# Attention into a two-layer MLP on one core: a new order of the first loads, weight conversions among the first heads, and four times as many products of zeros ahead of the fourth pair

## The chip, the cores and the metric

The kernel runs on one core of a Trainium2 chip. The metric is the device time of one execution in microseconds (us); a kernel's time is the median of its runs. Lower is better. Names used below: PE is the matrix engine (TensorE), ACT the scalar engine, DVE the vector engine, POOL the GpSimd engine, SP the engine whose queue issues nearly all loads and stores. PSUM is the memory of eight banks into which PE writes.

## The reference, cut to what matters

```python
# q, k, v: 8 batches, 8 heads, 576 positions, 64 per head, float32
scores = q @ k.T / 8                                   # per batch and head
mask_local   = (0 <= i - j) & (i - j < 32)             # heads 0 to 3
mask_strided = (0 <= i - j) & (i % 32 == j % 32)       # heads 4 to 7
attn = softmax(where(mask, scores, -1e9)) @ v
x = attn.transpose(0, 2, 1, 3).reshape(4608, 512)      # tokens x model
h = maximum(x @ w_in, 0)                               # 512 x 2048
y = (h * h) @ w_out                                    # 2048 x 512
```

All of it is float32 to the accuracy of float32.

## The kernel before, in words

The 4608 tokens are cut into 12 chunks of 384. For each chunk the attention of its tokens is written into four tiles: xlh and xll (local heads, high and low part), xsh and xsl (strided heads). A float32 number is split into a high part that the matrix engine takes as it is and a low part, the rest; a product of two such numbers is three matmuls. The MLP of a chunk walks over 16 tiles of the hidden layer. `up` (L430) makes a tile h of 128 hidden units by 384 tokens in 12 matmuls, four parts of x by three products; ACT then takes relu, square and the high part gh (L435, L436, L437), DVE the low part gl (L438). `down` (L450) adds the tile into three PSUM banks y in nine matmuls, six with gh and three with gl. PE works at `up` of tile s and `down` of tile s - 2 in turn, while the other engines do the attention of the next chunk: local heads by `pe_head` (L214 and L216 split keys and queries, L231 scores, L240 exponentials, L245 scaling, L273 products with v), strided heads on POOL and DVE (L380, L381, L402, L403).

The weights come in 16 pieces, alternately of w_in and w_out. `fetch(k)` loads piece k (the first twelve in one load of 1 MB, 128 x 1024 numbers of two words), and `convert()` makes its high and low part from two 32-bit words of each number: a scaling of the whole piece on ACT (L150), and then for each half an ACT pass into a PSUM bank (L162, into a bank of `zbank`), two DVE passes (L165, L166), an ACT cast (L169, the high part) and a POOL subtraction (L170, the low part). The cast and the subtraction of a half are written behind the ACT pass of the half after it.

Chunk 0 has nothing to overlap with, so its heads are worked out in four pairs by `pe_pair`: first[0] and first[1] are the local heads, late[0] and late[1] (the third and the fourth pair) the strided ones with their tokens sorted. A pair runs in steps, and a `next` of its generator writes one step: the loads of qk and v; the scores (L308, 8 products into two PSUM banks) with mask and row minimum on DVE (L312, L313); the subtraction on POOL (L316), exponential on ACT (L317), sum on DVE (L318), reciprocal (L320) and scaling on POOL (L322); the transposes on PE (L327) with their copies on ACT (L328); the products with v (L335 local, L346 strided); and the split into x (L350 on ACT, L351 on DVE). In the names below, b_0_1_200 and b_0_1_201 are the two banks of first[0], b_1_1 those of first[1], b_0_0 those of late[0] and b_1_0 those of late[1]; the e tiles are named in the same way, and the last number only tells tiles apart.

`zeros(bank, n)` (L525) has PE multiply zeros n times; nothing reads the result. Before the first pair it does 60 of these, after the first two pairs' scores 30, and ahead of the fourth pair's scores 30 more.

What sets the order: each engine works its own program in order. A scheduler places the instructions of the source into these programs by a model of durations, so the order in a program is not that of the source. `tc.issue_after(x)` and `behind(...)` keep what is written inside from being placed before x. Loads of SP's queue are issued in program order; the first loads hold, in KB, qk of a local pair 416, v of a local pair 256, qk of a strided pair 384, v of a strided pair 192, a piece of weights 1024, and on ACT's queue the masks 256 and the identity 64.

Of the kernel before, what the change touches and what calls it, by code (L numbers as in the profile page):

```python
# [12 lines left out]
ALU = mybir.AluOpType  # L13
AX = mybir.AxisListType
# [14 lines left out]
QC = 96  # L29
# [9 lines left out]
NWARM = 60  # L39

NEARLY = 3
# [6 lines left out]
def f32(ap):  # L48
    return ap.bitcast(F32)
# [11 lines left out]
def windows(c):  # L61

    res, at = [], 0
    for b, g in SEGS[c]:
        for qc in (2 * g, 2 * g + 1):
            if res and res[-1][:2] != (b, qc - 1):
                at += STR
            res.append((b, qc, at))
            at += QC
    return res  # L70
# [14 lines left out]
def attn_moe(ctx: ExitStack, tc, qk_l, v_l, qk_d, v_d, qk_p, v_p, f_s, q_s, k_s, v_s, w_in, w_out, masks, eye, out):  # L85
    nc = tc.nc
# [13 lines left out]
    def psum(i, nm):  # L100

        return ps.tile([P, 512], F32, name=nm, tag=f"ps{i}")
# [16 lines left out]
    last = {}  # L119
# [4 lines left out]
        order += [(p, 0), (p - 1, 1)]  # L124
    order.append((NFT // 2 - 1, 1))
    wi, wo, raws = {}, {}, {}
    zbank, zturn = (2, 3), iter(range(1000))

    def fetch(k):

        p, which = order[k]
        src = (w_out if which else w_in)[p].bitcast(U32).rearrange("p (n t) -> p n t", t=2)
        if k < 12:
            raw = wpool.tile([P, 1024, 2], U32, name=f"raw{k}", tag=f"w{k + 8 if k < 8 else k + 4}")
            nc.sync.dma_start(out=raw, in_=src)
            raws[k] = [(raw, slice(0, 1024))]
        else:
            raws[k] = []
            for i in range(0, 1024, WP):
                raw = spool.tile([P, WP, 2], U32, name=f"raw{k}_{i}", tag="s3", bufs=5)  # L140
                nc.sync.dma_start(out=raw, in_=src[:, i : i + WP])
                raws[k].append((raw, slice(i, i + WP)))
# [40 lines left out]
    def x_tiles(c):  # L183
        if c not in xt:
            xt[c] = {
                (kind, part): xpool.tile([P, 2, TC], F32R, name=f"x{kind}{part}{c}", tag=f"x{kind}{part}")
                for kind in "ls"
                for part in "hl"
            }
        return xt[c]  # L190
# [94 lines left out]
    def pe_pair(c, pr, local, qk, vr, es, pt, banks, sm):  # L285

        u = f"{c}_{pr}_{int(local)}"
        if local:
            kw, wins, nv = KW, [at for _, _, at in windows(c)], P
            src, vsrc = qk_d[c, pr], v_d[c, pr]  # L290
            mk = mask_sb[:QC, 0:2, :].rearrange("p w k -> p (w k)").unsqueeze(1).broadcast_to([QC, 2, 2 * KW])
        else:
            kw, wins, nv = QC, [QC * w for w in range(NW)], QC
            src, vsrc = qk_p[pr], v_p[pr]
            mk = mask_sb[:QC, 3, :QC].unsqueeze(1).broadcast_to([QC, NW, QC])
        nk = wins[-1] + kw
        nc.sync.dma_start(out=qk[:, : TC + nk], in_=src[:, : TC + nk])
        last["s"] = nc.sync.dma_start(out=vr[:nv], in_=vsrc)
        yield
        v4 = vr.rearrange("p (h w d) -> p h w d", h=2, w=NW)  # L300
        nm = small.tile([P, 2, NW], F32, name=f"nm{u}", tag="nm")
        rs = small.tile([P, 2, NW], F32, name=f"rs{u}", tag="rs")
        ss, s_ps = sums[sm], [banks() for _ in range(2)]
        e4 = [e[:QC, : NW * kw].rearrange("p (w k) -> p w k", k=kw) for e in es]
        for w in range(NW):
            for h in range(2):
                rows = slice(D * h, D * (h + 1))
                last["p"] = nc.tensor.matmul(s_ps[h][:QC, w * kw : (w + 1) * kw], qk[rows, w * QC : (w + 1) * QC], qk[rows, TC + wins[w] : TC + wins[w] + kw], start=True, stop=True)  # L308
        for h in range(2):

            flat = (lambda t: t[:, : NW * kw].rearrange("p (g k) -> p g k", g=mk.shape[1]))
            nc.vector.scalar_tensor_tensor(out=flat(es[h][:QC]), in0=flat(s_ps[h][:QC]), scalar=-SCALE, in1=mk, op0=ALU.mult, op1=ALU.subtract)  # L312
            nc.vector.tensor_reduce(out=nm[:QC, h], in_=e4[h], op=ALU.min, axis=AX.X)  # L313
        yield
        for h in range(2):
            nc.gpsimd.tensor_sub(e4[h], e4[h], nm[:QC, h].unsqueeze(2).broadcast_to([QC, NW, kw]))  # L316
            last["a"] = nc.scalar.activation(e4[h], e4[h], AF.Exp, scale=-1.0)  # L317
            nc.vector.tensor_reduce(out=ss[:QC, NW * h : NW * (h + 1), 0], in_=e4[h], op=ALU.add, axis=AX.X)  # L318
        nc.vector.tensor_reduce(out=rs[:QC].rearrange("p h w -> p (h w)"), in_=ss[:QC], op=ALU.add, axis=AX.X)
        last["v"] = nc.vector.reciprocal(rs[:QC], rs[:QC])  # L320
        for h in range(2):
            last["g"] = nc.gpsimd.tensor_mul(e4[h], e4[h], rs[:QC, h].unsqueeze(2).broadcast_to([QC, NW, kw]))  # L322
        yield
        p4 = pt.rearrange("p (h w q) -> p h w q", h=2, w=NW)
        for h in range(2):
            for w in range(NW):
                nc.tensor.transpose(s_ps[h][:kw, w * QC : (w + 1) * QC], e4[h][:, w], ident[:QC, :QC])  # L327
            last["a"] = nc.scalar.copy(pt[:kw, h * TC : (h + 1) * TC], s_ps[h][:kw, :TC])  # L328
        yield
        x = x_tiles(c)  # L330
        if local:
            o = s_ps[0]
            for w in range(NW):
                for h in range(2):
                    nc.tensor.matmul(o[D * h : D * (h + 1), w * QC : (w + 1) * QC], v4[:kw, h, w], p4[:kw, h, w], start=True, stop=True)  # L335
            outs = [(o[:, :TC], [x["l", s][:, pr, :] for s in "hl"])]
        else:

            r0 = D * pr
            outs = []  # L340
            for a in range(2):
                o = s_ps[a]
                for w in range(NW):
                    for h in range(2):
                        p0 = r0 + STR * h
                        nc.tensor.matmul(o[p0 : p0 + STR, w * QC : (w + 1) * QC], v4[:kw, h, w, STR * a : STR * (a + 1)], p4[:kw, h, w], start=True, stop=True)  # L346
                by_i = lambda t: t[r0 : r0 + D].rearrange("p (s i r) -> p s i r", s=2, r=STR)
                outs.append((o[r0 : r0 + D, :TC].rearrange("p (s r i) -> p s i r", s=2, i=SI), [by_i(x["s", s][:, a, :]) for s in "hl"]))
        for src, (xh, xl) in outs:
            last["a"] = nc.scalar.copy(xh, src)  # L350
            last["v"] = nc.vector.tensor_sub(xl, src, f32(xh))  # L351
        yield
# [109 lines left out]
    def behind(ins, gen):  # L462

        while True:
            with ExitStack() as st:
                for i in ins.values():
                    st.enter_context(tc.issue_after(i.ins))
                try:
                    k = next(gen)
                except StopIteration:  # L470
                    return
            yield k
# [39 lines left out]
    ungated = convert()  # L512

    late = [pair_at(0, pr, False, 2 + pr, ("y0", "14")[pr]) for pr in range(2)]
    first = [pair_at(0, pr, True, pr, ("23", "yy")[pr]) for pr in range(2)]
# [6 lines left out]
    def zeros(bank, n):  # L522
        w_ps = psum(bank, f"w_ps{bank}")
        for _ in range(n):
            nc.tensor.matmul(w_ps[:, :P], warm, warm, start=True, stop=True)  # L525

    zeros(0, NWARM)
    next(first[0])
    next(first[1])
    nc.scalar.dma_start(out=mask_sb, in_=masks)  # L530
    nc.scalar.dma_start(out=ident, in_=eye)
    next(late[0])
    next(late[1])
    for k in range(NEARLY):
        fetch(k)
    next(first[0])
    next(first[1])
    with tc.issue_after(last["p"].ins):
        zeros(0, NWARM // 2)
        for k in range(NEARLY, 8):  # L540
            fetch(k)
    next(late[0])
    with tc.issue_after(last["p"].ins):
        zeros(1, NWARM // 2)
    next(first[0])
    next(first[1])
    weights = behind({"a": last["a"]}, ungated)
    next(late[1])
    for i in range(2):
        next(first[0])  # L550
        next(first[1])
        next(late[0])
        next(late[1])
        if i:
            weights = behind({"a": last["a"]}, ungated)
        else:
            for _ in range(2 * NEARLY):
                next(weights)
    next(late[0])
    next(late[1])  # L560
# [1 line left out]
    zbank = (2,)  # L562

    NS = NCHUNK * NFT
    for s in range(NS + 2):
        c, j = divmod(s, NFT)
# [8 lines left out]
        if c + 1 < NCHUNK:  # L575
# [11 lines left out]
            while ds < fs * cost:  # L587
                k = next(st, "end")
# [82 lines left out]
```

## Time and profile before

| what | value |
|---|---|
| median of 3 runs | 903.63 us (903.14 to 903.86) |
| the profiled execution | 902.66 us |
| span of its instructions | 900.8 us |
| PE busy | 886.3 us, 98% |
| POOL, DVE, ACT busy | 693.4, 669.5, 564.4 us |
| TensorE clock granted, mean of the span | 0.982 |

The span runs from the first to the last instruction; the profiled execution is 1.86 us longer, and it is 0.97 us below the median. Busy shares are averages over the span; a wait shows as "idle before" an instruction, with the instruction that released it behind an arrow. A clock of 1.00 is full speed, 0.50 half.

### The profile page before, as it was taken

How to read it: one execution, taken by the hardware profiler on the slowest of the kernel's cores; microseconds unless marked ns; L12 is line 12 of the kernel's file. 1: busy time of each engine (PE TensorE's matmuls, PEld its weight loads, DVE VectorE, ACT ScalarE, POOL GpSimd, SP SyncE). 2: the span in 40 equal slices, each digit the busy share in tenths (PEclk: the TensorE clock that was granted, in tenths of full speed). 3: DMA queues.
4: the chain of work that ended last, by engine and by line, in shares of the span. 5: the costliest groups of instructions: out<-in, count | busy, mean ns of one | idle time of the engine just before them, and what ended most of it. 6: DMA issues, size and time to landing. Idle time of an engine off the chain costs nothing.

```text
span 900.8 us, 14866 instructions
## 1 busy us (share of the span) xinstructions
PE 886.3 (98%) x4744; PEld 800.0 (89%) x4744; DVE 669.5 (74%) x1840; ACT 564.4 (63%) x1458; POOL 693.4 (77%) x724
## 2 busy tenths in 40 slices
PE   8989999999999999999999999999999999999997
PEld 7778899999999999999989989999999999999996
DVE  6789668878877878878878887887886887885111
ACT  3898967657657657747746755755665765764332
POOL 5788577788788889989879997988899799785000
PEclk8599999999999999999999999999999999999999
DMA  9833441323113114102212311221131111000000
GB/s 352 346 123 126 129 150 35 121 69 104 51 51 112 47 48 139 43 13 98 75 32 69 104 31 54 59 86 60 28 110 47 46 46 68 25 1 2 35 1 35
DMA packets 26798, 71.41 MB, mean 79 GB/s; under 512 B 2976, under 2 KB 8736, under 8 KB 25184
## 3 DMA queue, kind: packets, MB, share of 16 engines
q1 hardware_dynamic: 26432, 70.14, 23.4%
q8 instruction: 37, 0.61, 0.3%
q10 hardware_dynamic: 288, 0.33, 0.1%
q14 instruction: 41, 0.34, 0.1%
HBM read 61.01 MB, written 9.44 MB: 78 GB/s over the span
## 4 chain that ended last, share of the span: by engine, by line
PE 86%; POOL 5%; DVE 5%; ACT 2%; issue 1%; DVEq 0%; POOLq 0%; ACTq 0%
PE h L430 41%; PE y L450 40%; POOL pp L402 2%; PE s L231 2%; PE o L273 2%; POOL pq L380 1%; DVE sc L381 1%; DVE px L263 1%; PE b L308 1%; DVE p_t L256 1%; PE w_ps L525 1%; PE b L335 0%; POOL kx L215 0%; DVE e L312 0%; DVE nm L313 0%
## 5 line engine op out<-in xcount | busy, mean ns | idle before, releaser
L450 PE MATMUL y<-w,gh 128*128 128x512 f32 x1152 | 361.9, 395 | 2.4 <-ACT gh L437 2.4
L450 PEld LDWEIGHTS y<-w,gh 128*128 128x128 f32 x1152 | 212.6, 189 | 35.0 <-ACT gh L437 2.6
L430 PE MATMUL h<-xlh,w 128*128 128x384 f32 x768 | 232.7, 342 | 0.4 <-DVE xsl L351 0.4
L430 PE MATMUL h<-xsh,w 128*128 128x384 f32 x768 | 228.1, 337 | 0.0
L402 POOL TENSOR_TENSOR pp<-vs,sc 128x448 f32<-128x448 f32 (+10 forms) x192 | 193.6, 1034 | 39.9 <-issue 21.7
L450 PE MATMUL y<-w,gl 128*128 128x512 f32 x576 | 223.7, 395 | 0.0
L380 POOL TENSOR_TENSOR pq<-ks,qs 128x512 f32<-128x512 f32 (+2 forms) x192 | 200.1, 1063 | 16.0 <-DVE sc L381 12.4
L381 DVE TENSOR_REDUCE sc<-pq 128x8 f32<-128x512 f32 (+4 forms) x228 | 120.1, 535 | 61.4 <-POOL pq L380 59.7
L435 ACT ACTIVATE h<-h 128x384 f32<-128x384 f32 x192 | 91.0, 475 | 112.6 <-PE h L430 111.5
L438 DVE TENSOR_TENSOR gl<-h,gh 128x384 fp32r<-128x384 f32 x192 | 105.4, 549 | 61.4 <-ACT gh L437 59.9
L430 PEld LDWEIGHTS h<-xlh,w 128*128 128x128 f32 x768 | 142.9, 189 | 8.4 <-DVE xsl L351 0.7
L430 PEld LDWEIGHTS h<-xsh,w 128*128 128x128 f32 x768 | 142.5, 189 | 0.5 <-ACT w L169 0.3
L403 DVE TENSOR_REDUCE qs<-pp 128x64 f32<-128x448 f32 (+11 forms) x192 | 106.8, 563 | 31.7 <-POOL pp L402 29.6
L430 PE MATMUL h<-xll,w 128*128 128x384 f32 x384 | 130.3, 339 | 0.0
L430 PE MATMUL h<-xsl,w 128*128 128x384 f32 x384 | 129.2, 336 | 0.0
L450 PEld LDWEIGHTS y<-w,gl 128*128 128x128 f32 x576 | 108.0, 188 | 20.8
L437 ACT CAST gh<-h 128x384 fp32r<-128x384 f32 x192 | 91.2, 475 | 34.1 <-PE y L450 30.3
L436 ACT ACTIVATE h<-h 128x384 f32<-128x384 f32 x192 | 91.0, 474 | 4.5
L240 ACT ACTIVATE e<-e,nm 96x128 f32<-96x128 f32 x160 | 62.6, 392 | 28.3 <-DVE nm L223 27.0
L430 PEld LDWEIGHTS h<-xll,w 128*128 128x128 f32 x384 | 72.8, 190 | 7.5
L256 DVE STREAM_TRANSPOSE p_t<-e 32x128 f32<-32x128 f32 x240 | 72.2, 301 | 4.8 <-ACT e L245 1.4
L430 PEld LDWEIGHTS h<-xsl,w 128*128 128x128 f32 x384 | 72.7, 189 | 0.2
(82 smaller groups left out, 1113.6 us busy)
## 6 DMA issues: line engine op xcount, KB each, us to landing
qk<-qk_l SPq DMA_DIRECT2D x24, 400.0 KB, 3.1
y<-ysb SPq DMA_DIRECT2D x36, 256.0 KB, 2.3
raw<-w_in SPq DMA_DIRECT2D x7, 1024.0 KB, 11.1
qk<-qk_l SPq DMA_DIRECT2D x16, 416.0 KB, 3.1
vs<-v_s SPq DMA_DIRECT2D x10, 576.0 KB, 3.8
raw<-w_out SPq DMA_DIRECT2D x5, 1024.0 KB, 13.3
v<-v_l SPq DMA_DIRECT2D x40, 128.0 KB, 2.0
ks<-k_s SPq DMA_DIRECT2D x8, 576.0 KB, 3.7
```

What stands on the lines that cost most here:

```text
L240: nc.scalar.activation(e[:QC, cut(w)], e[:QC, cut(w)], AF.Exp, bias=nmax[:QC, w : w + 1], scale=-1.0, accum_out=ssum[:QC, w, :1])
L256: nc.vector.transpose(out=pt[STR * k : STR * (k + 1), :, STR * r : STR * (r + 1)], in_=e.rearrange("p (w k) -> p w k", k=KW)[STR * r : STR ...
L380: nc.gpsimd.tensor_mul(pv, kt[:, a : a + m, :], qt[:, i - i0 : i - i0 + 1, :].broadcast_to([P, m, D]))
L381: nc.vector.tensor_reduce(out=sc[:, i - i0, a : a + m], in_=pv, op=ALU.add, axis=AX.X)
L402: nc.gpsimd.tensor_mul(pv, vt[:, a : a + nd, :n], sc[:, il : il + 1, :n].broadcast_to([P, nd, n]))
L403: nc.vector.tensor_reduce(out=ot[:, il, a : a + nd], in_=pv, op=ALU.add, axis=AX.X)
L430: nc.tensor.matmul(ph[:, :TC], w[:, wsl], xx, start=n == 0, stop=n == 11)
L435: nc.scalar.activation(g, g, AF.Relu)
L436: nc.scalar.activation(g, g, AF.Square)
L437: nc.scalar.copy(gh, g)
L438: nc.vector.tensor_sub(gl, g, f32(gh))
L450: nc.tensor.matmul(y_ps[c][t], g[:, sl], w[:, wsl], start=j == 0 and k == 0, stop=j == NFT - 1 and k == 2)
```

## The change

For chunk 0, a pair's v is now loaded by a step of its own. The loads come in the order qk, qk (first two pairs), weights piece 0, qk of late[0], v, v, weights piece 1, qk of late[1], v, v, weights piece 2. In before all eight loads of the pairs came ahead of the weights. Of the conversions' halves, two are now written right behind the last row minimum (L313) of first[1], and two more behind the softmax step of the first two pairs; in before all six of the first three pieces were written behind the last exponential of these pairs. Until the fourth pair's scores are written, the ACT pass of a conversion goes into PSUM bank 4 alone, one of the two banks of late[1], where it went into banks 2 and 3 before. There are 120 products of zeros ahead of the fourth pair in place of 30. Line numbers of after are two higher from L298 on (L308 is L310, L312 is L314, L316 is L318, L317 is L319, L318 is L320, L322 is L324, L327 is L329, L335 is L337, L430 is L432, L435 to L438 are L437 to L440, L450 is L452).

```diff
-    zbank, zturn = (2, 3), iter(range(1000))
+    zbank, zturn = (4,), iter(range(1000))
...
         nc.sync.dma_start(out=qk[:, : TC + nk], in_=src[:, : TC + nk])
+        if c == 0:
+            yield
         last["s"] = nc.sync.dma_start(out=vr[:nv], in_=vsrc)
...
-            nc.vector.tensor_reduce(out=nm[:QC, h], in_=e4[h], op=ALU.min, axis=AX.X)
+            last["m"] = nc.vector.tensor_reduce(out=nm[:QC, h], in_=e4[h], op=ALU.min, axis=AX.X)
...
     zeros(0, NWARM)
-    next(first[0])
-    next(first[1])
+
+    for h in first:
+        next(h)
     nc.scalar.dma_start(out=mask_sb, in_=masks)
     nc.scalar.dma_start(out=ident, in_=eye)
-    next(late[0])
-    next(late[1])
-    for k in range(NEARLY):
-        fetch(k)
+    fetch(0)
+    for h in (late[0], *first):
+        next(h)
+    fetch(1)
+    for h in (late[1], *late):
+        next(h)
+    fetch(2)
     next(first[0])
     next(first[1])
     with tc.issue_after(last["p"].ins):
         zeros(0, NWARM // 2)
         for k in range(NEARLY, 8):
             fetch(k)
+    weights = behind({"v": last["m"]}, ungated)
+    next(weights)
+    next(weights)
     next(late[0])
     with tc.issue_after(last["p"].ins):
-        zeros(1, NWARM // 2)
+        zeros(1, 2 * NWARM)
     next(first[0])
     next(first[1])
+    next(weights)
+    next(weights)
     weights = behind({"a": last["a"]}, ungated)
     next(late[1])
+    zbank = (2, 3)
     for i in range(2):
         next(first[0])
         next(first[1])
...
-            for _ in range(2 * NEARLY):
+            for _ in range(2 * NEARLY - 4):
                 next(weights)
```

The scheduler places the new conversions as follows. ACT's program of before, from its first exponential (L317) on; raw_192 is piece 0 of the weights, pt the transposed probabilities:

```order
L317 ACTIVATE e_0_1_111<-e_0_1_111 96x512
L317 ACTIVATE e_0_1_112<-e_0_1_112 96x512
L317 ACTIVATE e_1_1_116<-e_1_1_116 96x512
L317 ACTIVATE e_1_1_117<-e_1_1_117 96x512
L150 ACTIVATE raw_192<-raw_192 128x1024
L317 ACTIVATE e_0_0_100<-e_0_0_100 96x384 x2
L328 COPY pt_0_1_113<-b_0_1_200 128x384
```

The same place in after, where raw_186 is piece 0 and raw_191 piece 1, w_0_272 the converted piece 0:

```order
L150 ACTIVATE raw_186<-raw_186 128x1024
L162 ACTIVATE z_0_273<-raw_186 128x512
L319 ACTIVATE e_0_1_111<-e_0_1_111 96x512
L150 ACTIVATE raw_191<-raw_191 128x1024
L319 ACTIVATE e_0_1_112<-e_0_1_112 96x512
L319 ACTIVATE e_1_1_116<-e_1_1_116 96x512
L319 ACTIVATE e_1_1_117<-e_1_1_117 96x512
L162 ACTIVATE z_512_278<-raw_186 128x512
L169 CAST w_0_272<-raw_186 128x512
L319 ACTIVATE e_0_0_100<-e_0_0_100 96x384 x2
```

The scaling of piece 1 now stands between the first exponential and the three others of the local pairs, and the scaling of piece 0 ahead of all of them. On POOL two subtractions of weight halves (L170, of w_0_272) now stand ahead of the third pair's scaling: one between the subtractions (L318) and the scalings (L324) of the first two pairs, one behind those scalings. In before the first L170 came behind all six scalings and the two subtractions of the fourth pair. On DVE, the passes L165 and L166 over piece 0 now stand among the row minima and sums of the first three pairs.

PE's program of before, from the second half of the fourth pair's scores (b_1_0_340, behind the last zeros) on; the first half, b_1_0_341, stood ahead of those zeros:

```order
L308 MATMUL b_1_0_340<-qk_1_0_104 96x96 x4
L327 MATMUL b_0_1_200<-ident,e_0_1_111 128x96 x4
L327 MATMUL b_0_1_201<-ident,e_0_1_112 128x96 x4
L335 MATMUL b_0_1_200<-pt_0_1_113,v_0_1_110 64x96
L327 MATMUL b_1_1_216<-ident,e_1_1_116 128x96 x4
```

The same in after, from the fourth pair's first scores (b_1_0_457, behind the 120 products of zeros) on:

```order
L310 MATMUL b_1_0_457<-qk_1_0_104 96x96 x4
L329 MATMUL b_0_1_200<-ident,e_0_1_111 128x96 x4
L329 MATMUL b_0_1_201<-ident,e_0_1_112 128x96 x4
L337 MATMUL b_0_1_200<-pt_0_1_113,v_0_1_110 64x96
L329 MATMUL b_1_1_216<-ident,e_1_1_116 128x96 x4
L337 MATMUL b_0_1_200<-pt_0_1_113,v_0_1_110 64x96 x7
L329 MATMUL b_1_1_217<-ident,e_1_1_117 128x96 x4
L337 MATMUL b_1_1_216<-pt_1_1_118,v_1_1_115 64x96
L310 MATMUL b_1_0_458<-qk_1_0_104 96x96 x4
```

The second half of the fourth pair's scores, b_1_0_458, has moved behind the transposes of the first two pairs; it is the bank, number 4, that the conversions use until then.

The change also moves instructions far behind the start. ACT's program of before where chunk 10 begins, h_0_9133 being its tile 0:

```order
L435 ACTIVATE h_0_9133<-h_0_9133 128x384
L436 ACTIVATE h_0_9133<-h_0_9133 128x384
L437 CAST gh_0_9146<-h_0_9133 128x384
L435 ACTIVATE h_1_9192<-h_1_9192 128x384
L436 ACTIVATE h_1_9192<-h_1_9192 128x384
```

The same place in after, h_0_9223 being tile 0 of chunk 10:

```order
L437 ACTIVATE h_0_9223<-h_0_9223 128x384
L240 ACTIVATE e_0_9253,sums_94<-e_0_9253,nm_0_9319 96x128 x2
L437 ACTIVATE h_1_9282<-h_1_9282 128x384
L438 ACTIVATE h_0_9223<-h_0_9223 128x384
L437 ACTIVATE h_2_9358<-h_2_9358 128x384
L438 ACTIVATE h_1_9282<-h_1_9282 128x384
L245 ACTIVATE e_0_9253<-e_0_9253,rs_0_9320 96x128 x4
L214 CAST kx_2_9574<-qk_2_9568 128x416
L216 CAST qx_2_9573<-qk_2_9568 128x384
L439 CAST gh_0_9236<-h_0_9223 128x384
```

Relu, square and cast of tile 0 stood together in before; in after eleven other instructions stand between its relu and its cast (L439, which makes gh). In PE's program of after, ten products of tiles 1 and 2 and four of scores stand behind the last product of tile 0, and then the first product that reads gh of tile 0.

## The prediction

> **What bounds the kernel now.** The windows view comes first: one long stretch from 52 us to near the end. Its columns are the stretch, its length, busy time and count of PE, weight loads, DVE, ACT and POOL, the granted TensorE clock, the busy share of the DMA engines and GB/s.
>
> ```profile
> 52.00:895.00 843.00, 841.64 (x4385) 762.16 (x4384) 632.04 (x1766) 530.45 (x1399) 660.23 (x680) 1.00 0.20 65
> ```
>
> PE is busy 841.64 of 843 us at full clock. The waits of PE in that stretch are one line:
>
> ```profile
> PE o L273 <- DVE px L263: 1.3, 1, 1.3
> ```
>
> So a change moves the end in two ways only: by moving the moment at which this dense stream begins, and by opening holes in it. The chain of waits shows how the stream begins (start, us, what):
>
> ```profile
> 33.18 2.29 PE h L430 x6
> 35.47 2.71 PE b L346 x32
> 38.17 1.95 PE b L308 x8
> 40.12 5.38 PE h L430 x16
> ...
> 49.23 2.93 PE y L450 x6
> 52.16 2.12 PE h L430 x12
> ```
>
> The first product of the MLP starts at 33.18, the first y at 49.23, and the stream is dense from 52.16, with the third h tile. Ahead of 33.18 the chain is the softmax of the four pairs. I read it in the timeline of each engine; the bracket is the idle time before and its releaser. ACT first:
>
> ```profile
> 11.49 0.63 ACT L317 ACTIVATE e<-e 96x512 f32<-96x512 f32 x1 [0.36 <-POOL e L316]
> 12.88 0.63 ACT L317 ACTIVATE e<-e 96x512 f32<-96x512 f32 x1 [0.76 <-POOL e L316]
> 14.07 0.63 ACT L317 ACTIVATE e<-e 96x512 f32<-96x512 f32 x1 [0.56 <-POOL e L316]
> 15.38 1.14 ACT L150 ACTIVATE raw<-raw 128x1024 f32<-128x1024 f32 x1 [0.69 <-DMA raw<-w_in]
> 16.41 1.08 ACT L317 ACTIVATE e<-e 96x384 f32<-96x384 f32 x2
> ```
>
> The second exponential is at 11.49; the first piece of weights has landed at 15.38, and its scaling takes 1.14 us. POOL next, then PE:
>
> ```profile
> 16.89 5.60 POOL L322 TENSOR_TENSOR e<-e,rs 96x512 f32<-96x512 f32 x6
> 22.45 1.60 POOL L316 TENSOR_TENSOR e<-e,nm 96x384 f32<-96x384 f32 x2
> ```
>
> ```profile
> 12.71 1.85 PE L525 MATMUL w_ps<-p_t 128*128 128x128 bf16 x30
> 14.62 0.92 PE L308 MATMUL b<-qk 64*96 64x96 f32 x8
> 17.98 1.90 PE L327 MATMUL b<-ident,e 96*128 96x96 f32 x8 [2.45 <-POOL e L322]
> ...
> 23.46 0.58 PE L335 MATMUL b<-pt,v 128*64 128x96 f32 x2
> 23.97 1.52 PE L327 MATMUL b<-ident,e 96*96 96x96 f32 x8
> ```
>
> PE waits 2.45 us for the scaling on POOL, which starts at 16.89. The fourth pair's scores (the row at 14.62) are done long before; DVE, which computes the reciprocals at 18.46, takes their second half at 20.05:
>
> ```profile
> 18.46 0.20 DVE L320 RECIPROCAL rs<-rs 96x8 f32<-96x8 f32 x1
> ...
> 20.05 0.54 DVE L312 SCALAR_TENSOR_TENSOR e<-b,mask_sb 96x384 f32<-96x384 f32 x1
> ```
>
> **The change part by part.** I follow one chain from the loads to the dense stream, and then look behind it. Four groups give the conversions' prices (last figures: busy us, mean ns of one), and three windows the loads and the clock:
>
> ```profile
> L170 POOL TENSOR_TENSOR w<-raw,w 128x512 fp32r<-128x512 f32 x32 | 42.2, 1323 | 18.7 <-ACT w L169 18.7
> ...
> L165 DVE SCALAR_TENSOR_TENSOR z<-raw,z 128x512 uint32<-128x512 uint32 x32 | 22.1, 691 | 10.3 <-ACT z L162 9.9
> L166 DVE SCALAR_TENSOR_TENSOR raw<-raw,z 128x512 uint32<-128x512 uint32 x32 | 21.9, 685 | 0.9
> ```
>
> ```profile
> 0.00:15.36 15.36, 13.50 (x184) 12.72 (x184) 7.89 (x14) 4.02 (x6) 5.71 (x15) 1.00 0.91 320
> 14.60:18.00 3.40, 0.93 (x9) 0.77 (x9) 3.14 (x10) 2.16 (x4) 2.72 (x4) 1.00 1.01 419
> 28.00:30.00 2.00, 2.00 (x28) 2.00 (x29) 1.93 (x6) 2.00 (x4) 1.12 (x1) 0.50 0.97 406
> 45.50:49.00 3.50, 1.37 (x10) 0.91 (x9) 2.09 (x5) 3.48 (x8) 1.48 (x2) 0.96 0.29 79
> ```
>
> *Loads, and the scaling of piece 1 on ACT.* In ACT's new program the scaling of piece 1 stands ahead of the second exponential, so three exponentials are queued behind a load, and DVE's sums, POOL's scalings and PE's transposes behind them. When does piece 1 land? In before piece 0 landed at 15.36 with 3840 KB issued up to it (832 of qk, 512 of v, 768 and 384 of the strided pairs, 320 of masks and identity, 1024). In after 4096 KB are issued up to piece 1 (832, 1024, 384, 512, 320, 1024): 256 KB more, 0.63 us at the 419 GB/s of 14.6 to 18, so 16.0 at the latest. At the earliest, with nothing behind it sharing the engines, 4.19 MB at the 320 GB/s of the first 15.36 us give 13.1. I take 15.4, nearer to the first, since loads behind piece 1 share the engines here as there. With the scaling of 1.14 the second exponential starts at 16.5 in place of 11.49: **+5.0** (+2.8 to +5.7).
>
> *To the scaling of the first pair on POOL.* From the second exponential to 16.89 there are 5.40 us in before. In after, behind that exponential, DVE has two sums, L166, the third pair's two row minima, two sums and L165 in its way, and POOL the third pair's second subtraction and one L170. The exponential ends at 17.1. DVE then needs about 0.6 and 0.6 for the sums (512 columns, where L312 takes 0.54 for 384), 0.69 for L166 and 1.1 for the two minima (384 columns): 20.1. POOL: subtraction 0.80 (half of the row at 22.45), L170 1.32: 22.2, so the scaling starts at about **22.3, +5.4**. L170 is worth 1.3 of that; if POOL can fit it into its idle time, +4.1.
>
> *To the fourth pair's second scores on PE.* In before the transposes start 1.09 us behind the scaling, and transposes and products with v take 6.06 us from 17.98 to 24.04 (the row at 23.46 ends there). In after these stand ahead of the second half of the fourth pair's scores: 22.3 + 1.1 + 6.1 = 29.5. The four scores take half of the 0.92 of eight, twice that at half clock, 0.9, and one pass of DVE's queue another 0.6: DVE takes them at 31.0, against 20.05.
>
> *To the first h.* In before 13.1 us lie between 20.05 and 33.18, conversions among them on every engine. In after the bare chain is mask 0.54, minimum 0.54, subtraction 0.80, exponential 0.54, sum 0.54, a small sum and the reciprocal 0.2 each, two scalings 1.6 and eight transposes at about 1.5 (the row at 23.97): 6.5; one conversion step on DVE (0.69) and part of one on POOL make it 8.2. First h at **39.2, +6.0**. Bounds: the bare chain with the early load, 35.3; with one more L170 and DVE step in the way, 41.2.
>
> *From the first h to the dense stream.* PE's own work between, 2.29 + 2.71 + 1.95 + 5.38 = 12.3, stays. The rest up to the first y, 3.7 us in before, is relu, square and cast of ACT in a queue with conversions: ACT is busy 3.48 of 3.50 us there, PE 1.37. With two pieces converted early some of these are gone, but the rows of the second tile stand closer: I take −0.5 (−2 to 0.5). The first y and the third h then lie in a later clock window: 2.93 was at half clock in part, −0.7 (−0.7 to 0). The dense stream starts at 57.0 in place of 52.16: **+4.8** (1 to 7).
>
> *The 120 products of zeros.* 90 more by 1.85/30 are 5.6 us of PE, from about 12 to 19.5, in time in which PE would wait for POOL until 23.4 anyway: nothing. If the transposes were ready at 17.98 as before, the zeros would delay them by 1.5. The clock is what they may touch. It was full up to 18.0; PE was busy 0.93 of 3.4 us before that, and then the clock was half. In 28 to 30 PE is busy 2.00 of 2.00 and stays at 0.50; in 45.5 to 49, behind the h products, it is 0.96. In after the zeros end at about 19.5 and PE waits to 23.4, so the same fall, one window later. The Trainium skill, "TensorE: Matmul & The Clock Gate", Part 1, has the clock rise after one busy window of about 3.4 us; by that the small products would have raised it at once, which the row at 28 to 30 does not bear out. Its price is a rival below.
>
> *Chunk 10.* The scheduler's new order opens a hole in the dense stream. Behind relu of tile 0, ACT has relu, square and scaling work to do before gh. Prices from a steady stretch, where relu and exponentials follow each other every 0.39:
>
> ```profile
> 764.94 0.47 ACT L435 ACTIVATE h<-h 128x384 f32<-128x384 f32 x1 [1.15 <-PE h L430]
> 765.33 0.39 ACT L240 ACTIVATE e<-e,nm 96x128 f32<-96x128 f32 x1
> ...
> 768.74 1.28 ACT L245 ACTIVATE e<-e,rs 96x128 f32<-96x128 f32 x4 [0.70 <-DVE rs L242]
> ...
> 771.74 0.54 ACT L214 CAST kx<-qk 128x416 fp32r<-128x416 f32 x1 [0.22 <-PE s L231]
> 772.18 0.51 ACT L216 CAST qx<-qk 128x384 fp32r<-128x384 f32 x1
> ```
>
> Seven passes of 0.39 (three relus, two squares, two exponentials), 1.28, twice 0.44 and the cast 0.47 are 5.36, with the handovers 5.6 to 5.8. PE has meanwhile ten h products at 2.12/12 and four of scores of 256 columns, 0.12 each by the 384 of an h product: 2.2. PE waits **3.6** for gh of tile 0 (0, if a later part of the order absorbs it, to 5.5, if it costs a window of the clock too, as the window 45.5 to 49 did).
>
> *Later pieces of weights.* They are converted beside chunk 0 and are wanted at a fixed distance behind its tiles, both 4.8 us later; that hides them. I put **+0.5** for holes in this cover (−1.3, if PE's one wait of 1.3 goes, to 1.5).
>
> **Sum:** 4.8 + 3.6 + 0.5 = 8.9. Against the profiled execution of 902.66 (span 900.8 and 1.86 around it) 911.6; the median stood 0.97 above the profiled one, so 912.5 by it. I write 912.0.
>
> **The rivals.** *Other side: the zeros keep the clock up.* If small products count as busy for the gate and the 120 zeros bridge the wait, PE runs from 18 to 45 at full clock. The half of 2.71 + 1.95 + 5.38 + 2.93 = 13.0 us, 6.5, would come off, and the start-up would be −1.7 instead of +4.8; with the hole of chunk 10 that gives 905.1, and without the hole 901.5. [...] Against it: the row at 28 to 30, and the wait of 4 us that I find. 0.12, half of it without the hole; neither half is slower by what can be told.
>
> *The hole of chunk 10 costs nothing,* as ACT could be ahead of PE there: 911.6 − 3.6 gives 908.5. For it: only that ACT's queue is a plan; against: ACT's program is in fixed order, and each relu waits for PE. 0.12.
>
> *Piece 1 lands early,* at 13.1: the first h is 2 to 2.5 earlier, 909.8. 0.15. *Everything is slower than summed* (more conversions on the chain, a further clock window lost): above 915. 0.10.
>
> **How the numbers follow.** My forecast, start-up +4 to +6 and a hole of 3 to 5, holds 0.51: 910 to 914.5. Cases below, down to the full clock with the hole, reach 904.5; leaving out 0.06 below 904.5 and 0.10 above 915 keeps 8 in 10. A measurement of this kernel can tell some 0.2%, 1.8 us. Faster needs full clock and no hole: half of the first rival, 0.06. Within 0.2% (901.8 to 905.4): its other half, and 0.04 for a clock that is full in some windows only, beside a small hole: 0.10. Slower: the rest, 0.84.
>
> **What would show it.** In the profile of after: the second exponential waits for a load of weights, to about 16.5; the first POOL scaling at 22.3; second scores of the fourth pair at 29.5; first h at 39.2; first y at 54.8; dense from 57; a wait of PE y for ACT gh of 3 to 4 us where chunk 10 begins (around 750 us). Wrong would be: the clock at 1.00 between 22 and 45; no wait of ACT for a load among the local exponentials; no new wait of PE behind 57.

## The result, and the profile after

The changed kernel takes 913.28 us (median of 4 runs, 911.95 to 914.09) against 903.63: the ratio is 1.0106, 95% interval 1.0089 to 1.0124, so it is slower by about 1.1%. The profiled execution took 912.61 us, with a span of 910.8; in before these were 902.66 and 900.8. The 10 us of the two spans are what is accounted for here.

The first chain went as forecast. ACT's timeline of after among the local pairs' exponentials:

```profile
11.82 0.63 ACT L319 ACTIVATE e<-e 96x512 f32<-96x512 f32 x1 [1.58 <-POOL e L318]
15.39 1.14 ACT L150 ACTIVATE raw<-raw 128x1024 f32<-128x1024 f32 x1 [2.94 <-DMA raw<-w_in]
16.44 1.66 ACT L319 ACTIVATE e<-e 96x512 f32<-96x512 f32 x3
```

The scaling of piece 1 waits 2.94 us for its load, and three exponentials wait behind it. POOL's timeline, and the chain of waits from the first h on:

```profile
21.07 1.29 POOL L170 TENSOR_TENSOR w<-raw,w 128x512 fp32r<-128x512 f32 x1
22.32 4.04 POOL L324 TENSOR_TENSOR e<-e,rs 96x512 f32<-96x512 f32 x4
```

```profile
38.98 1.99 PE h L432 x6
40.97 1.59 PE b L348 x32
42.56 1.04 PE b L310 x8
43.60 3.01 PE h L432 x16
...
50.91 2.47 PE y L452 x6
53.38 2.85 PE h L432 x12
56.23 2.09 PE y L452 x9
```

First POOL scaling at 22.32 (before 16.89), first h at 38.98 (33.18). But the four steps that follow take 7.6 us where they took 12.3, and the first y is at 50.91, only 1.7 behind before. The windows view of after says why:

```profile
24.00:26.00 2.00, 1.59 (x8) 1.15 (x9) 1.61 (x3) 1.63 (x4) 2.00 (x3) 0.54 1.02 426
38.00:40.00 2.00, 2.00 (x11) 1.98 (x10) 0.55 (x1) 1.50 (x5) 0.53 (x2) 0.50 0.98 344
40.00:42.00 2.00, 2.00 (x28) 1.56 (x28) 1.39 (x2) 1.75 (x4) 1.31 (x1) 0.69 0.16 56
42.00:44.00 2.00, 2.00 (x25) 1.71 (x22) 1.42 (x4) 1.79 (x4) 0.01 (x1) 1.00 0.15 39
```

The granted clock falls at 24.2 and is back at 41.2. In before it was still half there, and came back at 45.3:

```profile
40.00:42.00 2.00, 2.00 (x7) 1.95 (x7) 1.77 (x5) 0.01 (x1) 1.92 (x3) 0.50 0.85 309
```

Behind the start the waits of PE in after (total, times, longest, from 56 us on) are three groups:

```profile
PE y L452 <- ACT gh L439: 3.4, 1, 3.4
PE o L273 <- DVE px L263: 1.3, 3, 0.5
PE y L452 <- POOL w L170: 0.4, 1, 0.4
```

The first is the hole where chunk 10 begins. ACT's timeline there, then PE's:

```profile
768.95 0.43 ACT L438 ACTIVATE h<-h 128x384 f32<-128x384 f32 x1
769.31 0.44 ACT L437 ACTIVATE h<-h 128x384 f32<-128x384 f32 x1
769.68 0.44 ACT L438 ACTIVATE h<-h 128x384 f32<-128x384 f32 x1
770.05 1.27 ACT L245 ACTIVATE e<-e,rs 96x128 f32<-96x128 f32 x4
771.22 0.53 ACT L214 CAST kx<-qk 128x416 fp32r<-128x416 f32 x1
771.65 0.52 ACT L216 CAST qx<-qk 128x384 fp32r<-128x384 f32 x1
772.06 0.48 ACT L439 CAST gh<-h 128x384 fp32r<-128x384 f32 x1
```

```profile
768.59 0.64 PE L231 MATMUL s<-kx,qx 128*96 128x256 f32 x4
772.59 2.93 PE L452 MATMUL y<-w,gh 128*128 128x512 f32 x6 [3.37 <-ACT gh L439]
```

PE waits 3.37 us for the cast at the end of ACT's row, and then works at half clock: six y products in 2.93 us, twice the 1.39 of full clock, and in 774 to 778 the granted clock is 0.50 with PE busy all the time:

```profile
770.00:774.00 4.00, 1.41 (x3) 1.16 (x4) 3.88 (x19) 4.00 (x15) 3.79 (x4) 0.71 0.07 29
774.00:778.00 4.00, 4.00 (x12) 3.38 (x11) 3.88 (x11) 2.93 (x12) 3.92 (x5) 0.50 0.01 2
778.00:782.00 4.00, 4.00 (x20) 3.60 (x19) 3.83 (x9) 1.57 (x4) 2.65 (x3) 0.94 0.00 0
```

The clock falls at 771.7, when PE has been idle for 2.5 us, and is back at 778.5, 6.8 us later; 0.9 us of the wait lie behind the fall. By the Trainium skill, "TensorE: Matmul & The Clock Gate", Part 1, the clock halves after one idle window of about 3.4 us and comes back after one busy one. The trace agrees with the length, 6.8 us being two such windows, but not with a window that has to be idle throughout: PE still worked in the 3.4 us ahead of the fall.

How far one execution lags behind another at a time is best read from the products still to come, as the order of the products differs. At 750 us the windows view gives for the h and the y products of before

```profile
750.00:930.00 180.00, 75.54 (x395) 69.67 (x393) 0.99 0.05 17
750.00:930.00 180.00, 80.18 (x315) 58.13 (x315) 0.99 0.05 17
```

and for those of after

```profile
750.00:930.00 180.00, 78.44 (x405) 72.23 (x404) 0.97 0.06 21
750.00:930.00 180.00, 83.03 (x324) 61.25 (x324) 0.97 0.06 21
```

Ten h at 0.177 us (2.12/12 in the chain of before) and nine y at 0.232 (2.09/9 in that of after) make 3.9 us of lag. Small products count 0.12. In this way, against the profiled execution of before, in us (the kernels are those of the experiments below; a negative lag is a lead):

| kernel | at 62 | at 131 | at 750 | at 850 |
|---|---|---|---|---|
| after | 2.1 | 3.5 | 3.9 | 10.2 |
| nohole | 1.4 | 3.0 | 3.0 | 6.0 |
| nohole2 | 1.6 | 3.0 | 4.5 | 10.7 |
| late_scale | 5.1 | 5.0 | 7.5 | 7.7 |
| z30 | 5.3 | 5.3 | 7.8 | 8.2 |
| noconv | 1.7 | 2.1 | 6.3 | 6.2 |
| loads | 0.9 | 0.9 | 1.1 | 1.1 |
| bz120 | 1.2 | 1.7 | 4.2 | 4.2 |
| late_conv | 3.8 | 3.6 | 5.1 | 5.1 |
| ghfirst | -1.0 | 5.1 | 4.0 | 10.7 |
| b_ghfirst | -2.9 | 6.0 | 7.1 | 14.5 |
| a_relief | 1.4 | 3.0 | 3.3 | 3.3 |
| b_relief | 0.9 | 0.9 | -0.5 | -0.4 |

Executions of one program differ in it: after, nohole, nohole2 and a_relief, the same up to 62, lie between 1.4 and 2.1. The profiled execution of before is itself an early one. Its first exponential starts at 10.50, and at 11.36 in b_relief, whose edit begins only in chunk 4 and which stands at 0.9 in the table; loads, which takes the time of before, stands at 0.9 too. A lag below 1 us therefore says nothing, and of the 2.1 that after loses at the start up to 0.9 can be this execution of before. Then come 1.4 up to 131, where the only wait of PE listed is for a half of the weights (0.4), some 0.4 on the way, and 6.4 at chunk 10.

### The profile page after: what moved, and what is told of

Its sections match the earlier page's. It is cut to its first block, busy times and chain, and to the rows that moved or that the text cites. A ratio compares the mean times of both kernels' runs of the same rounds, so it can differ in the third digit from the quotient of the medians.

```text
span 910.8 us, 15025 instructions
## 1 busy us (share of the span) xinstructions
PE 892.6 (98%) x4834; PEld 804.6 (88%) x4834; DVE 673.6 (74%) x1840; ACT 562.2 (62%) x1458; POOL 692.7 (76%) x724
## 4 chain that ended last, share of the span: by engine, by line
PE 84%; DVE 6%; POOL 5%; ACT 2%; DMA 2%; issue 1%; DVEq 0%; POOLq 0%; ACTq 0%
PE h L432 39%; PE y L452 39%; PE s L231 2%; PE o L273 2%; POOL pp L404 1%; DMA raw<-w_in 1%; DVE p_t L256 1%; POOL pq L382 1%; DVE px L263 1%; PE b L337 1%; DVE gl L440 1%; PE b L329 1%; DVE qs L405 1%; PE b L310 1%; PE b L348 0%
## 5 line engine op out<-in xcount | busy, mean ns | idle before, releaser
L452 PE MATMUL y<-w,gh 128*128 128x512 f32 x1152 | 361.7, 396 | 6.8 <-ACT gh L439 6.3
L452 PEld LDWEIGHTS y<-w,gh 128*128 128x128 f32 x1152 | 213.1, 189 | 41.0 <-ACT gh L439 6.7
L432 PE MATMUL h<-xlh,w 128*128 128x384 f32 x768 | 232.8, 343 | 0.0
L432 PE MATMUL h<-xsh,w 128*128 128x384 f32 x768 | 227.0, 335 | 0.0
L452 PE MATMUL y<-w,gl 128*128 128x512 f32 x576 | 223.7, 396 | 0.0
L432 PEld LDWEIGHTS h<-xlh,w 128*128 128x128 f32 x768 | 143.2, 190 | 8.7 <-DVE gl L440 0.7
L437 ACT ACTIVATE h<-h 128x384 f32<-128x384 f32 x192 | 90.8, 474 | 97.2 <-PE h L432 96.5
L440 DVE TENSOR_TENSOR gl<-h,gh 128x384 fp32r<-128x384 f32 x192 | 105.2, 548 | 59.3 <-ACT gh L439 55.6
L432 PEld LDWEIGHTS h<-xsh,w 128*128 128x128 f32 x768 | 141.6, 188 | 0.7 <-POOL w L170 0.3
L432 PE MATMUL h<-xll,w 128*128 128x384 f32 x384 | 130.8, 341 | 0.0
L432 PE MATMUL h<-xsl,w 128*128 128x384 f32 x384 | 128.7, 335 | 0.0
L452 PEld LDWEIGHTS y<-w,gl 128*128 128x128 f32 x576 | 108.4, 188 | 21.4
L439 ACT CAST gh<-h 128x384 fp32r<-128x384 f32 x192 | 91.4, 476 | 32.2 <-PE y L452 27.0
L438 ACT ACTIVATE h<-h 128x384 f32<-128x384 f32 x192 | 91.0, 474 | 4.4
L432 PEld LDWEIGHTS h<-xll,w 128*128 128x128 f32 x384 | 73.0, 190 | 7.1
L432 PEld LDWEIGHTS h<-xsl,w 128*128 128x128 f32 x384 | 72.1, 188 | 0.1
```

Of the source, the lines that this page charges most:

```text
L432: nc.tensor.matmul(ph[:, :TC], w[:, wsl], xx, start=n == 0, stop=n == 11)
L437: nc.scalar.activation(g, g, AF.Relu)
L438: nc.scalar.activation(g, g, AF.Square)
L439: nc.scalar.copy(gh, g)
L440: nc.vector.tensor_sub(gl, g, f32(gh))
L452: nc.tensor.matmul(y_ps[c][t], g[:, sl], w[:, wsl], start=j == 0 and k == 0, stop=j == NFT - 1 and k == 2)
```

## The experiments

Ratios are to before, with their 95% intervals.

**nohole.** The changed kernel; what is written for chunk 11's local heads stays behind the cast of tile 0 of chunk 10.

```diff
-        nc.scalar.copy(gh, g)
+        casts[c, j] = nc.scalar.copy(gh, g)
...
+            hold = {"h": casts[c, 0]} if c == 10 and j == 0 else {}
+            if hold:
+                lo = behind(hold, lo)
```

> The changed kernel with one constraint more: the first attention step of chunk 11 (its keys and queries) is not placed before the cast of tile 0 of chunk 10; nothing is left out and the program is the same up to about 740 us. Theory A (of the 10 us lost, 2.1 are the start, 1.4 late weights, and 6.4 the wait of 3.4 for gh at 769 us with the two half-clock windows behind it): no wait over 1 us there, clock 1.00, 906.9 (905.9 to 907.9). Rival B (ACT's work only comes later, and PE waits for it elsewhere): another wait of 2 to 4 us behind 770, 910 to 913.

908.74 us, 1.0056 (1.0044 to 1.0068). The lag does not grow in chunk 10 (3.0 at 750, 2.9 at 800), so the stretch on ACT was that hole. But 3 us come back in chunk 11, where PE waits for the strided heads' tiles, which ACT and POOL make (L415, L416), 1.1 us each; the clock stays full there. Theory A had the place, and not the sequel; rival B was right by half.

**nohole2.** The same with `j == 1` in place of `j == 0`, so that fewer steps are held back.

> The changed kernel with the constraint of the first such run put one tile later: only what is written from the exponentials of the first head of chunk 11 on stays behind the cast of tile 0 of chunk 10; keys and queries of that head may come earlier. One instruction stands between relu and cast of tile 0 besides its own square. Theory A (the stretch on ACT is the hole, and the second hole of the run before came from holding back the keys): no wait over 1 us from 760 us to the end, shift at the end that of after at 750 us, +3.9, and 907 (906 to 908). Rival B (what POOL has to do for chunk 11 makes a hole in chunk 11 whenever PE does not wait in chunk 10): again 2 to 3 us lost at 820 to 845, 909.

913.37 us, 1.0106 (1.0090 to 1.0123), as slow as after. No loss in chunk 10, and 6.1 in chunk 11. Its waits of PE from 10 us on:

```profile
PE h L432 <- ACT xsh L415: 1.9, 1, 1.9
PE h L432 <- POOL xsl L416: 1.0, 1, 1.0
```

The clock is half from 839.1 to 845.9, which is most of what sets the 6.1 us apart from the 3 of nohole. So taking the wait out of chunk 10 moved the loss by one chunk, and rival B holds. What is late there is POOL. Busy times from 820 us to the end follow the length in the order PE, weight loads, DVE, ACT, POOL. In nohole2 POOL has 16.69 us left, in before 3.35:

```profile
820.00:930.00 110.00, 83.38 (x402) 74.44 (x400) 22.95 (x43) 29.27 (x61) 16.69 (x16) 0.96 0.04 15
```

```profile
750.00:930.00 180.00, 145.69 (x742) 131.50 (x740) 70.04 (x186) 69.11 (x174) 63.35 (x62) 0.99 0.05 17
820.00:930.00 110.00, 75.69 (x377) 67.88 (x375) 14.39 (x26) 26.88 (x56) 3.35 (x3) 0.98 0.04 15
```

At 750 us POOL of after is 11.0 us behind before, and PE only 3.9:

```profile
750.00:930.00 180.00, 152.52 (x761) 137.29 (x760) 79.09 (x203) 71.35 (x180) 74.32 (x74) 0.97 0.06 21
```

It is 2.5 us behind at 60, 4.7 at 200, 3.8 at 300, 8.5 at 500: its lag grows over the stream, though not evenly. That POOL's lag makes the hole was theory D, tried next.

**a_relief.** The changed kernel, with one POOL pass per chunk (L248) on ACT from chunk 4 on.

```diff
-        if h != HL - 1:
+        if h != HL - 1 or c >= 4:
```

> The changed kernel with one scaling of the softmax, of the fourth local head, on ACT instead of POOL for the chunks 4 to 11: eight of the ten 1.04 us passes leave POOL, 8.3 us, and ACT does four of 0.32 each for it as for the other heads. The start and the order up to chunk 3 stay; in chunk 10 its order has no long stretch between relu and cast. Theory D, formed on the runs so far (POOL, 11 us behind before at 750 us while PE is 3.9 behind, is what PE pays for at the end, in chunk 10 or 11, whichever the order picks): POOL's lag shrinks to about 3 us, no hole in chunk 10 or 11, shift at the end 3.9 (3 to 5), 907.5 (906 to 909). Rival (the hole is a matter of ACT's order alone, and POOL's lag was hidden): a hole of 3 us or more in chunk 11 as with the two constraints, 910 to 913.

906.46 us, 1.0033 (1.0021 to 1.0045): no hole in chunk 10 or 11, lag 3.3 to the end. POOL's lag did not shrink as far as I had said: 9.0 at 750, but 11.0 us of work are left at 820 in place of 16.69, and PE no longer waits for it:

```profile
820.00:930.00 110.00, 78.97 (x395) 70.85 (x393) 20.58 (x39) 29.91 (x64) 11.00 (x11) 0.99 0.04 15
```

So the hole went although POOL's lag hardly shrank, from 11.0 to 9.0 where theory D asked for 3, and the edit changed the order of ACT in chunk 10 too: its forecast of the time came true, its mechanism is not shown. What speaks for it is a comparison over all kernels run. By the busy time that POOL has left at 750 us beyond that of before, the five that lose 3 us or more in chunk 10 or 11 are 10 us or more behind (nohole 10.2, after 11.0, nohole2 11.3, ghfirst 12.0, b_ghfirst 14.1), and all others less (a_relief 9.0, noconv 6.4, bz120 4.8, the rest 2.0 at most). That goes together; no run moved POOL's lag alone.

**b_relief.** The same edit to before.

> The kernel before with the same scaling on ACT for the chunks 4 to 11, as a control. Theory D: in before POOL keeps pace, so nothing is to be gained: shift 0 +- 1, 903.5 (902.5 to 905). Rival (POOL holds PE up in before too): 1 us or more faster, 902.

902.20 us, 0.9983 (0.9974 to 0.9992). The time is the rival's: between 500 and 600 us, where before's one wait of 1.3 for DVE was, the lag goes from 0.7 to -1.1. That POOL held PE up there is not shown, as the wait of before names DVE's pass L263, which took 2.89 us at that place and 0.54 in b_relief. It beats both kernels, by little.

**z30.** `zeros(1, NWARM // 2)` in place of `zeros(1, 2 * NWARM)` in the changed kernel.

> The changed kernel with 30 products of zeros ahead of the fourth pair in place of 120, all else as in the change. Its order keeps the scaling of piece 1 ahead of the second exponential and the second scores behind the transposes, and has no long stretch at chunk 10. Theory A (the zeros cost nothing by themselves): second exponential at 16.4, first h at 38.5 to 39.5, clock half from 18 in place of 25.8, and without the hole 907 (906 to 908.5). Rival (the zeros are what delays the start): first h at 33 to 35, 902 to 904.

910.77 us, 1.0086 (1.0073 to 1.0098). First h at 37.5, against 38.7 in after by the same view, PE's timeline; 0.5 of that is a load that came earlier (second exponential 15.95). So the zeros cost the first h under 1 us, and not the 4 us and more of the rival. But the first y is at 53.66 and the lag at 62 is 5.3 in place of 2.1: the 120 zeros do not cost 3 us, they come with a start that is 3 us shorter. The waits of PE from 10 us on:

```profile
PE y L452 <- ACT gh L439: 6.5, 2, 6.0
PE b L329 <- POOL e L324: 5.1, 1, 5.1
```

There is no hole in chunk 10, and the sum still came out 3.8 above the forecast. Where the clock fell (16.8 in place of 24.2) and how the conversions lie in ACT's queue both differ; which of the two makes the 3 us stays open.

**late_scale.** In the changed kernel, the scaling of piece 1 behind the first two pairs' last exponential.

```diff
+            if k == 1:
+                with tc.issue_after(last["a"].ins):
+                    scale(1)
...
-                if not at and k + 1 < NFT and k + 1 in raws:
+                if not at and k and k + 1 < NFT and k + 1 in raws:
```

> The changed kernel with the scaling of weights piece 1 written behind the exponentials of the first two pairs; the early conversions, the load order, bank 4 and the 120 products of zeros stay. Its order has no long stretch between relu and cast of a tile in chunk 10. Theory A (the start is late because three exponentials are queued behind the load of piece 1): second exponential at 12.5 in place of 16.4; POOL's first scaling still waits for a subtraction of weights whose cast stands behind that scaling, so it comes at 20.0 in place of 22.3, first h at 36.7; 904.6 (903 to 906). Rival B (the fourth pair's second scores, in bank 4 behind the transposes, make the start late): first h stays at 38.5 to 39, 906.9.

909.59 us, 1.0072 (1.0059 to 1.0085). Second exponential at 12.49, first POOL scaling at 20.60, first h at 37.5: the start of the chain went as A said, and it is 1.4 us earlier than in after, so the wait for the load accounts for only a part of the 5.8 us. But the first y is at 53.50, 2.6 later than in after, and the lag at 62 is 5.1. Neither A nor B had that. Its waits of PE show the place:

```profile
PE y L455 <- ACT gh L442: 5.9, 1, 5.9
```

**late_conv.** Besides, all but the first half's ACT pass of the early conversions behind POOL's scaling of the first two pairs.

```diff
     weights = behind({"v": last["m"]}, ungated)
     next(weights)
-    next(weights)
...
+    weights = behind({"g": last["g"]}, ungated)
     next(weights)
     next(weights)
+    next(weights)
```

> The changed kernel with the scaling of piece 1 and all but the first half's ACT pass written behind the POOL scaling of the first two pairs: exponentials, sums and scalings of these pairs have nothing of the weights between them but a first scaling and pass; loads, bank 4 and 120 zeros stay. Its order has no long stretch in chunk 10. Theory A as predicted (the dense stream follows the first h): second exponential 12.5, first POOL scaling 17.5, zeros until 19.5, first h at 35 (34 to 36.5), first y 4 us earlier than 50.9, at 47, dense stream 2 us ahead of before. Theory C, formed on the runs so far (the first y hangs on the queue of conversions on ACT, DVE and POOL, and the time of the first h only decides how much of that queue lies ahead of it): first h at 35, first y still at 49.5 to 53, shift of the dense stream +1 to +5.

907.27 us, 1.0041 (1.0028 to 1.0054). Its chain of waits:

```profile
33.56 2.29 PE h L435 x6
...
52.47 2.48 PE y L455 x6
```

The first h is 5.4 us earlier than in after, and the first y 1.6 later: theory C. The time of the first h does not set the dense stream. The clock behaved otherwise, too: it fell at 22.3, behind waits of 0.63 and twice 0.45 us, and was back at 25.7 with nothing but small products on PE.

**noconv.** The changed loads and 120 zeros, conversions as before (the four early `next(weights)` left out, `zbank` and the loop as before).

> The changed loads and the 120 products of zeros, but conversions as before (all six halves behind the last exponentials, banks 2 and 3). Theory A: exponentials and POOL's scalings as in before (second exponential at 11 to 12, first scaling at 16.5 to 17); the zeros now end behind the scaling, at 19.5, so the transposes start at about 20.0 in place of 17.98 and first h comes at 35 (34 to 36). With the clock falling at 21 to 25 as in the change: 904.5 (903 to 906). Rival (small products keep the clock once it is up, if PE never waits): clock 1.00 up to the first y, and 898 to 900.

906.52 us, 1.0038 (1.0026 to 1.0050), above the range of theory A and far from that of the rival; the profiled execution took 908.75. The first h came at 31.7, earlier than I said, and the first y again at 50.3 (PE's timeline):

```profile
31.67 0.66 PE L432 MATMUL h<-xlh,w 128*128 128x384 f32 x1 [4.09 <-DVE xsl L353]
...
50.33 2.49 PE L452 MATMUL y<-w,gh 128*128 128x512 f32 x6 [3.00 <-ACT gh L439]
```

The clock stayed full through the small products, which ended at 27.6, and fell only at 30.4, inside the gap that follows them:

```profile
18.00:20.00 2.00, 2.00 (x31) 1.80 (x28) 1.35 (x6) 0.51 (x1) 2.00 (x3) 1.00 1.01 418
26.00:28.00 2.00, 1.51 (x30) 1.29 (x30) 0.70 (x2) 2.00 (x5) 0.92 (x1) 1.00 1.04 434
28.00:30.00 2.00, 0.00 (x0) 0.00 (x0) 1.85 (x3) 2.00 (x5) 0.38 (x1) 1.00 0.99 412
32.00:34.00 2.00, 1.94 (x6) 1.27 (x5) 1.96 (x6) 1.98 (x4) 1.17 (x2) 0.50 1.02 406
```

That bought nothing: PE then waits 4.09 us for the split of x. A hole of 4 us lies between 200 and 300 us (lag 2.3 and 6.3).

**bz120.** 120 zeros in the kernel before, nothing else.

> The kernel before with 120 products of zeros ahead of the fourth pair in place of 30, nothing else. Theory A (the zeros end some 2 us behind the point at which the transposes were ready, but keep the clock up, and the first y hangs on ACT's queue and not on the first h): first y at 50 to 50.5, shift of the dense stream +1.5 as with the loads and the zeros together, and no gain from the clock; with a hole of 4 us in chunk 2, whose order is that of the run with loads and zeros, 908. Rival (the clock that stays up shortens the start): shift -1 to -2.

906.95 us, 1.0041 (1.0026 to 1.0056). First h 31.4, first y 50.03, lag 1.2 at 62; 2.4 us more are lost between 200 and 300 us. No gain from the clock, as theory A had it; its sum was 1 us too high. Ninety products of zeros at 13 us lose time at 250.

**loads.** The load order alone: noconv with 30 zeros.

> The kernel before with the changed order of loads alone (conversions as before, 30 products of zeros). Its order far behind the start is that of before. Theory A (the load order by itself costs and gives nothing, since the heads still come first and the conversions start where they did): first y at 49 to 49.5, shift of the dense stream 0 +- 0.7, 903.7 (903 to 904.5). Rival (weights that land earlier are converted earlier and the start gains): first y at 47 to 48, 902.

903.60 us, 1.0003 (0.9994 to 1.0012): nothing, as A had it. Its profiled execution has a span 1.0 longer than that of before, which is the lag in the table; the medians agree.

**ghfirst.** The changed kernel with the conversions beside tile 0 of chunk 0 behind its cast.

```diff
+        if s == 0:
+            weights = behind({"h": casts[0, 0]}, weights)
```

> The changed kernel with the conversions that stand beside tile 0 of chunk 0 placed behind its cast gh. Theory A (the first y waits for ACT's queue of conversions between square and cast, 2.9 us, and not for the first h): first y 2.5 to 3 earlier, 48; first h as in the change or up to 1 us earlier; dense stream earlier than in before by 0.5 to 1.5, unless the later weights open holes of their own between 60 and 130 us, which I put at 1 to 3. Rival (first y hangs on DVE or on PE): first y stays within 1 us of 50.9. The hole of chunk 10 is smaller in its order (8 instructions between relu and cast of tile 0): 0 to 4 us.

913.64 us, 1.0112 (1.0094 to 1.0131). First y at 48.99, 1.9 earlier, lag at 62 -1.0: the first y did wait for ACT's queue of conversions. By 131 us the lag is 5.1, more than the 1 to 3 allowed for: conversions that are put off are waited for later. The hole of chunk 10 is there, 6 us.

**b_ghfirst.** The same constraint in the kernel before.

> The kernel before with the same constraint, conversions beside tile 0 of chunk 0 behind its cast gh, and nothing else. Its order has the stretch of chunk 10 of the changed kernel (12 instructions between relu and cast of tile 0), although nothing of the change is in it. Theory A (the hole is a matter of the order that the scheduler falls into, and not of the change's parts): a wait of 3 to 4 us for gh where chunk 10 begins and two windows at half clock, +6.4 there; first y 2 to 2.5 earlier than 49.2; in all 907 to 909. Rival (a hole needs the late start of the change): no such wait, 901 to 903.

916.40 us, 1.0138 (1.0123 to 1.0153). The start gains 2.9, the later weights cost 8.9, and between 750 and 850 us 7.4 are lost, with a wait for gh of 3.7 us (PE's waits from 130 us on):

```profile
PE y L450 <- ACT gh L437: 3.7, 1, 3.7
```

So the hole of chunk 10 needs no part of the change; theory A's claim for it holds, its total was 8 us too low.

## Why the prediction was right, and where its steps failed

The forecast was 912.0 in 904.5 to 915.0, and 913.28 came. The sum for the profiled execution was 8.9 us, 10.0 came. That it came so near is luck: the start was put 2.7 us too high and the hole of chunk 10 2.8 too low, and the two errors cancelled. That the kernel would be slower, and in which two places, was not luck.

- *Loads to the first h: right to 0.3 us at each step.* Second exponential 16.44 (forecast 16.5), first POOL scaling 22.32 (22.3), second scores on DVE 31.11 (31.0), first h 38.98 (39.2). Zeros: forecast as no delay of the chain, and by z30 under 1 us; the clock fell at 24.2 in place of 18.0.
- *From the first h to the dense stream: wrong.* The step that failed is "PE's own work between, 12.3, stays". It took 7.6, since the clock was back at 41.2 and not at 45.3. The prediction let the clock rise at the same distance behind the first h. The first y came at 50.91 and not at 54.8, and the lag of the dense stream is 2.1 and not 4.8, of which up to 0.9 is the early execution of before. Beneath this lies a second error: that the dense stream follows the first h at all. Over the kernels run, first h ranges from 31.4 to 39.0 and first y from 48.2 to 53.7, without one following the other (late_conv 33.56 and 52.47, after 38.98 and 50.91).
- *The hole of chunk 10: wait right, price too low.* PE waited 3.37 (3.6), but the two windows at half clock behind it cost another 3.0, so 6.4; the upper bound of 5.5 was too low.
- *Later weights:* 1.4, within the bounds of -1.3 to 1.5, near their end.
- *The rival with the clock up* did not come about in after. In noconv and bz120 the clock did stay full over the small products and fell only at 30.4 and 29.8. My reading of the row at 28 to 30 said more than it can: it is shorter than a window of the clock, and shows a half clock with PE busy, not that small products cannot raise or hold it. In late_conv they raised it at 25.7. And the 6.5 us that I priced the rival at were not there to win: PE then waits for others.
- *What I did not see:* the hole of chunk 10 is not the scheduler's order alone. It is shown that without the stretch on ACT the loss comes in chunk 11 (nohole by half, nohole2 in full), where PE waits for what POOL and ACT make, and that it is gone in a_relief. That POOL's growing lag is the cause is argued from its busy time left, and from the comparison over all kernels; a_relief did not settle it. Why POOL falls behind from chunk to chunk in after was not settled; late_conv, which also makes early conversions, has no such lag (63.02 us left at 750, before 63.35).

Of the 10 us, then, 1 to 2 are lost at the start, 1.4 beside chunk 0 while the later weights are converted, and 6.4 far from the change, in chunk 10, where the new order makes PE wait; that the order alone is to blame for the loss is not shown, since without this wait nohole2 lost as much in chunk 11.

## What to carry to other kernels

Where a scheduler orders the program by modelled durations, a change at the start is priced in two parts: its own stage, and what the new order does to stages that it does not touch; here the second was two thirds of the loss, and ninety products of zeros were enough to set it off. A wait removed is a gain only if the engine behind it keeps pace: in nohole2 PE's wait went from one chunk to the next, with POOL 11 us behind. Price a hole in a dense PE stream with the half clock behind it, nearly double the wait here; in nohole, where two waits of 1.1 us left the clock full, it was 3 us for 2.2 of waiting. And do not take the first product of a stage for its pace before the other engines' queues have been counted.

## What the runs showed of the hardware

- A busy PE is not enough to raise the granted clock, and small products can both hold and raise it. They kept it full from 18 to 27.6 us in noconv, and in late_conv it rose at 25.7 with PE busy on them alone (3.20 of 3.20 us from 22.4 to 25.6). In before PE was busy with the same kind of products for 8.40 of 8.50 us from 18.0 on, and for 12.00 of 12.00 from 33.2 to 45.2 with 128 x 384 products among them, all at 0.50. What sets these stretches apart no run here shows.
- A wait of 3.37 us in a dense stream was followed by half clock up to 778.5, and cost 6.4 us in all. The clock had fallen before the wait was over, 2.5 us behind the last product.
